# Turning the last two query batches on VectorE, and cutting later loads into rows, in a fused attention and two-MLP kernel

## The chip, the cores and the metric

One core of one Trainium2 chip runs the whole program. The metric is the device time of one execution in microseconds. Three runs of the kernel before gave 1151.23, 1151.44 and 1151.57 us.

## The reference, cut to what matters

```python
# q, k, v: (4, 8, 576, 64); phi: (4, 8, 576, 32)
a = softmax(phi over the sequence)
k_m, v_m = einsum(a, k), einsum(a, v)            # 32 memory slots a head
attn = softmax(scale * q @ k_m.T)
x = (attn @ v_m), heads side by side              # (2304, 512)
h = x @ w_in;  x = leaky_relu(h, 0.01) @ w_out    # w_in, w_out are float64
p = domain_probs / domain_probs.sum(-1)
out = sum over 4 experts of p[:, e] * (relu(x @ w1[e]) @ w2[e])
```

## The kernel before, in words

The program has three stages. **Attention** goes batch by batch, four batches, named 0 to 3 here. A batch takes phi's maxima with a tree of four VectorE additions (`tree`, L548), turns them with two TensorE transposes (L552, L558), subtracts (L560) and exponentiates on ScalarE (L563). It turns its queries with 20 TensorE transposes (L576), whose results ScalarE or VectorE copy out of PSUM (L344). It forms the 32 memory keys and values with 72 small matmuls (L607; L596 for the values of batch 0), sums the weights with a second tree (L548, the z tree) and one matmul (L619), turns keys and values (L662, L658), and then, for each half s of the tokens, makes scores with 16 small matmuls (L685) and a softmax on VectorE (transposes out of PSUM L697, maxima L704, L706, exponent L709, sums L711, L713, L717, transposes back L720). The probabilities are split into a rounded high part and a low part (L344, L347); these are the tokens `ah`, `al`.

**The first MLP** folds the memory values into w_in: `y_pair` (L976) makes a y, which ACT and DVE split (L344, L347). `moe1_step` multiplies tokens and y in six matmuls (L960; for the first two steps three and three), applies the leaky rectifier (L1015), splits (L344, L347) and does twelve matmuls with w_out (L1027 to L1029). Its weights are float64 in memory and come as pieces of 512 values a partition, two 32-bit words a value. `piece64` makes float32 of them: a high part on ScalarE (L861) shifted on DVE (L879), a low part (L865 on ScalarE, L867 on DVE), the sign put into the low word (`signs`, L873 on DVE), and an addition on GpSimd (L878).

**The second MLP** (L1136 to L1206) takes the rest, from about 390 us on.

While attention runs, a region `xx` of four rows of 2304 words a partition holds the loads: `X0` to `X3` are its four quarters, each 576 words in each of the four rows. Keys, values and the queries of batch 1 live there; `A0` is elsewhere and holds the other queries. The fourth to seventh weight piece (`more0` to `more3`) is also kept in `xx`, one in each row, in words 1152 to 2175, that is in X2 and X3. Values of batch 1 go to X1.

The order on every engine comes from a planner (`Plan.issue`): each step has an engine, a cost and a due time, and a list scheduler writes them out; a table `SHIFTS` moves the due times of numbered steps. While TensorE has nothing in the plan during the first 50 us, the planner writes filler matmuls (L481) on the unit matrix. The engines run in that order, and wait on semaphores that a recorder adds from what the steps read and write. DMAs take eight semaphores, DMAHW0 to DMAHW7, in turn, and one that takes a semaphore waits for the DMA that had it last.

Of the kernel before, what the change touches and what calls it, by code (L numbers as in the profile page):

```python
# [11 lines left out]
F32R = mybir.dt.float32r  # L12
U32 = mybir.dt.uint32
F16 = mybir.dt.float16
AF = mybir.ActivationFunctionType
ALU = mybir.AluOpType
# [171 lines left out]
def kernel(  # L188
# [26 lines left out]
    HG = 4  # L215
# [314 lines left out]
    def att_batch(b):  # L530
# [10 lines left out]

        def tree(fold, rows):
            h = rows.shape[1]
            half = [tops[:, 0:n * P].rearrange("p (h r m) -> p h r m", h=h, r=n) for n in (4, 2, 1)]
            pairs = [(half[0], rows[:, :, 0:4], rows[:, :, 4:8]), (half[1], half[0][:, :, 0:2], half[0][:, :, 2:4]),
                     (half[2], half[1][:, :, 0:1], half[1][:, :, 1:2]), (half[2], half[2], rows[:, :, 8:9])]
            for out, in0, in1 in pairs:
                nc.vector.tensor_tensor(out=out, in0=in0, in1=in1, op=fold)  # L548
        op("DVE", 1.75, due, lambda: tree(ALU.max, rows), ["pl"], ["aT1"], two=True)
# [16 lines left out]
        due = yield  # L566
        for part in range(3):
            pairs = range(2 * part, min(2 * part + 2, (LT + 1) // 2))
            rows_, n = P if part < 2 else D, len(pairs) * HG * P
            pq = Banks(psum, (n + 511) // 512)  # L570

            def fn(pq=pq, pairs=pairs, rows_=rows_):
                for i, pair in enumerate(pairs):
                    for h in range(HG):
                        at_p = (i * HG + h) * P
                        nc.tensor.transpose(  # L576
                            pq[at_p:at_p + P][0:rows_], home(qn)[:, h, 2 * pair * D:2 * pair * D + rows_], ident)
            op("PE", 0.11 * len(pairs) * HG + 0.1, due, fn, [qn, "ident"], [pq], room=[f"qT{part}"])
            op("ACT", act(n), due, lambda e, pq=pq, pairs=pairs, rows_=rows_, n=n: copy(
                e, qT[0:rows_, pairs[0]:pairs[-1] + 1].rearrange("p r h n -> p (r h n)"), pq[0:n][0:rows_]),  # L580
               [pq], [f"qT{part}"], also=("DVE", dve(n)))

        for names in (("k",), ("v",)) if b == 0 else (("k", "v"),):
# [7 lines left out]
            def fn(pkv=pkv, src=src, n=len(names), wide=wide):  # L591
                for r in range(LT):
# [11 lines left out]
                    for h in range(HG):  # L604
                        for g in range(NGB):
# [7 lines left out]
                            )  # L613
            op("PE", 4.3 if wide else 1.0 + 0.6 * len(names), due, fn, ["a"] + [HOME[nm][b] for nm in names], [pkv])
            if "k" in names:
                op("DVE", 1.75, due, lambda: tree(ALU.add, a.rearrange("p r h m -> p r (h m)").unsqueeze(1)),
                   ["a"], ["aT1"], two=True)
                pz = Banks(psum, 1)
# [33 lines left out]
            for nm in names:  # L652
                pk = Banks(psum, 1)

                def fn(pk=pk, nm=nm):
                    if nm == "v":
                        for g in range(NGB):
                            nc.tensor.matmul(pk[0:P][g * D:(g + 1) * D], lhsT=kv[:, g, 1], rhs=ident, start=True, stop=True)  # L658
                        return
                    for x in range(2):  # L660
                        for g in range(NGB):
                            nc.tensor.matmul(pk[g * P:(g + 1) * P][x * D:(x + 1) * D],  # L662
                                             lhsT=kv[:, g, 0], rhs=ident, start=True, stop=True)
                n = 2 if nm == "k" else 1
# [8 lines left out]
        for s in range(2):  # L673
# [4 lines left out]
            def fn(ps=ps, s=s):  # L678
                for g in range(NGB):
                    for h in range(HG):  # L680
                        for x in range(2):
                            n = (LT + 1 - x) // 2
                            at_x = x * 512 + g * n * M
                            rs = slice(x * D, (x + 1) * D)
                            nc.tensor.matmul(  # L685
                                ps[at_x:at_x + n * M][h * M:(h + 1) * M].rearrange("p (r t) -> p r t", t=M),
                                lhsT=kb[rs, g, h * M:(h + 1) * M],
                                rhs=qT[rs, 0:n, h, (2 * g + s) * M:(2 * g + s + 1) * M],
                                start=True,
                                stop=True,  # L690
                            )
            op("PE", 0.7, due, fn, ["qT0", "qT1", "qT2", "kb"], [ps], [f"at{s}"])
# [7 lines left out]
            op("DVE", dve(S) + 0.15, due, fn, [ps, f"one{s}"], [f"at{s}"])  # L700
            at_r = at_[:, :, 0:M]
# [143 lines left out]
    def piece64(kind, n, sl, src, due, key, after):  # L845
# [23 lines left out]
        def signs(e):  # L869
            if e == "ACT":  # L870
                nc.scalar.mul(raw.bitcast(F16)[..., 1::4], high.bitcast(F32), 2.0 ** -112)
            else:
                nc.vector.scalar_tensor_tensor(  # L873
                    out=low, in0=high, scalar=0x80000000, in1=low, op0=ALU.bitwise_and, op1=ALU.bitwise_or
                )

# [4 lines left out]
        plan.op("ACT", 0.57, due, rest, [], [rk], also=("DVE", 0.5), two=True)  # L881
        plan.op("DVE", 0.7, due, signs, [], [rk], also=("ACT", 1.36), two=True)
        plan.op("POOL", 1.3, due, lambda e: add(e, fu), [rk], [fk], also=("DVE", 1.0), two=True)
# [78 lines left out]
    def y_pair(t, m, n):  # L962
# [25 lines left out]
        plan.op("PE", 0.45 * n - 0.1, t, fn,  # L988
                [key for i in range(n) for key in w_keys("w1", p + i)] + [f"vt{b * NGB + g}" for g in range(NGB)],
# [304 lines left out]
```

## Time and profile before

| | |
|---|---|
| median of 3 runs | 1151.44 us (1151.23 to 1151.57) |
| profiled execution, its own time | 1151.32 us |
| its span, first to last instruction | 1149.5 us |
| mean granted TensorE clock | 0.996 |
| busy: PE / DVE / ACT / POOL | 1127.0 / 676.2 / 440.5 / 98.2 us |
| HBM read / written | 125.60 / 34.08 MB |

Busy times are sums over an engine's instructions. PE counts matmuls, PEld the weight loads that overlap them. A busy PE is not a PE at its peak, since its fillers count, and since a matmul at half clock takes twice as long. The chain of waits follows the work back from the last instruction.

### The profile page before, as it was taken

The page shows a single profiled execution, that of the slowest core. Times are in us where ns is not written, and L with a number is a line of the kernel's source. Part 1 is how long each engine was busy: PE and PEld are TensorE (multiplying, and loading weights), DVE is VectorE, ACT ScalarE, POOL GpSimd, SP SyncE. Part 2 cuts the span into 40 slices and gives each one's busy share as a digit, 9 for nine tenths or more (in the row PEclk, how much of TensorE's full clock was granted, in tenths as well). Part 3 has the DMA queues.
Part 4 walks back from the last instruction along what each step waited for, and adds up shares of the span by engine and source line. Part 5 has one row for each costly group of instructions (what it writes and reads, how often), then busy time and mean ns, then how long its engine had stood idle before and what let it go on. Part 6 is the DMA issues. An engine that isn't in the chain of part 4 may idle for free.

```text
span 1149.5 us, 18174 instructions
## 1 busy us (share of the span) xinstructions
PE 1127.0 (98%) x7420; PEld 1020.6 (89%) x7420; DVE 676.2 (59%) x1279; ACT 440.5 (38%) x893; POOL 98.2 (9%) x102
## 2 busy tenths in 40 slices
PE   7699999999999999999999999999999999999998
PEld 4579999999999998989898998999998989998897
DVE  5776475843345787668677644455376644454543
ACT  5555567743434544433333323222124223222220
POOL 2431125510000000000000000000000000000000
PEclk9899999999999999999999999999999999999999
DMA  9555013310000377444544644433344553344402
GB/s 349 203 180 161 1 38 130 111 38 1 2 19 17 104 272 278 163 163 196 201 183 147 193 174 165 160 136 130 152 165 165 156 205 131 140 165 165 165 19 56
DMA packets 54104, 160.86 MB, mean 140 GB/s; under 512 B 6148, under 2 KB 22532, under 8 KB 47876
## 3 DMA queue, kind: packets, MB, share of 16 engines
q1 hardware_dynamic: 48836, 100.19, 24.8%
q0 software_dynamic: 4608, 58.72, 14.4%
q8 instruction: 58, 0.95, 0.3%
q10 hardware_dynamic: 576, 0.79, 0.2%
q14 instruction: 26, 0.21, 0.1%
HBM read 125.60 MB, written 34.08 MB: 139 GB/s over the span
## 4 chain that ended last, share of the span: by engine, by line
PE 95%; DMA 2%; DVE 2%; issue 0%; SPq 0%; ACT 0%; POOL 0%; DVEq 0%
PE psum L1136 31%; PE psum L1206 12%; PE psum L1205 12%; PE psum L1204 11%; PE psum L960 9%; PE psum L1027 6%; PE psum L1029 6%; PE psum L1028 6%; PE psum L976 1%; DMA exact<-in_moe_w_out_dram 1%; DMA exact<-in_v_dram 1%; PE psum L576 1%; PE psum L607 1%; PE psum L685 0%; DVE exact L873 0%
## 5 line engine op out<-in xcount | busy, mean ns | idle before, releaser
L1145 DVE TENSOR_TENSOR exact<-psum,exact 128x384 f32<-128x384 f32 x336 | 184.1, 556 | 272.0 <-PE psum L1136 269.6
L1152 ACT ACTIVATE rounded<-exact 128x384 fp32r<-128x384 f32 x192 | 100.9, 525 | 292.8 <-DVE exact L1145 291.0
L347 DVE TENSOR_TENSOR rounded<-exact,rounded 128x288 fp32r<-128x288 f32 (+3 forms) x223 | 123.5, 569 | 102.7 <-ACT rounded L344 101.9
L1206 PE MATMUL psum<-late,rounded 128*128 128x512 f32 x384 | 150.7, 392 | 0.0
L1205 PE MATMUL psum<-late,rounded 128*128 128x512 f32 x384 | 150.5, 392 | 0.0
L1204 PE MATMUL psum<-late,rounded 128*128 128x512 f32 x384 | 149.3, 389 | 0.0
L1136 PE MATMUL psum<-rounded 128*128 128x384 f32 x768 | 143.6, 336 | 0.1
L1136 PEld LDWEIGHTS psum<-rounded 128*128 128x128 f32 x768 | 134.8, 188 | 3.1 <-DVE exact L1145 1.0
L960 PE MATMUL psum<-rounded 128*128 128x288 f32 x768 | 125.4, 300 | 7.9 <-DVE rounded L347 7.9
L960 PEld LDWEIGHTS psum<-rounded 128*128 128x128 f32 x768 | 110.1, 191 | 14.0 <-issue 11.7
L344 ACT CAST rounded<-exact 128x288 fp32r<-128x288 f32 (+2 forms) x240 | 115.2, 500 | 14.1 <-DVE exact L820 3.9
L1027 PE MATMUL psum<-rounded 128*128 128x288 f32 x384 | 115.7, 301 | 0.0
L1029 PE MATMUL psum<-rounded 128*128 128x288 f32 x384 | 113.2, 295 | 2.3 <-issue 2.3
L1028 PE MATMUL psum<-rounded 128*128 128x288 f32 x384 | 113.2, 295 | 0.0
L1136 PE MATMUL psum<-late,rounded 128*128 128x384 f32 x576 | 109.7, 336 | 0.0
L1156 DVE SCALAR_TENSOR_TENSOR rounded<-exact,rounded 128x384 fp32r<-128x384 f32 x192 | 98.8, 550 | 12.9 <-ACT rounded L1152 12.9
L1136 PEld LDWEIGHTS psum<-late,rounded 128*128 128x128 f32 x576 | 102.0, 188 | 3.8
L1015 ACT ACTIVATE exact<-psum 128x288 f32<-128x288 f32 x128 | 52.6, 411 | 131.2 <-PE psum L960 126.6
L1167 ACT COPY exact<-psum 128x384 f32<-128x384 f32 x48 | 23.1, 481 | 196.8 <-PE psum L1136 196.8
L1206 PEld LDWEIGHTS psum<-late,rounded 128*128 128x128 f32 x384 | 72.0, 188 | 15.1
L1205 PEld LDWEIGHTS psum<-late,rounded 128*128 128x128 f32 x384 | 72.0, 188 | 13.4
L1204 PEld LDWEIGHTS psum<-late,rounded 128*128 128x128 f32 x384 | 72.1, 188 | 13.2
(113 smaller groups left out, 1664.6 us busy)
## 6 DMA issues: line engine op xcount, KB each, us to landing
rounded<-kept POOLq DMA_DIRECT2D x22, 1792.0 KB, 7.6
exact<-in_moe_w_dram SPq DMA_DIRECT2D x64, 512.0 KB
kept<-rounded SPq DMA_DIRECT2D x10, 1792.0 KB
w<-kept POOLq DMA_DIRECT2D x10, 1792.0 KB, 7.5
kept<-w SPq DMA_DIRECT2D x6, 1792.0 KB
exact<-in_moe_w_in_dram SPq DMA_DIRECT2D x16, 512.0 KB
exact<-in_moe_w_out_dram SPq DMA_DIRECT2D x16, 512.0 KB
exact<-in_k_dram SPq DMA_DIRECT2D x4, 1152.0 KB
```

The costliest lines, as they stand in the source:

```text
L344: nc.scalar.copy(out, in_) if e == "ACT" else engine(e).tensor_copy(out, in_)
L347: engine(e).tensor_tensor(out=out, in0=in0, in1=in1, op=ALU.subtract)
L960: nc.tensor.matmul(ps, lhsT=l, rhs=r, start=start and n == 0, stop=stop and n == len(seq) - 1)
L1027: nc.tensor.matmul(po, lhsT=w2l[:, ds_], rhs=th, start=first, stop=False)
L1028: nc.tensor.matmul(po, lhsT=w2h[:, ds_], rhs=tl, start=False, stop=False)
L1029: nc.tensor.matmul(po, lhsT=w2h[:, ds_], rhs=th, start=False, stop=last)
L1136: nc.tensor.matmul(ps[k][0:TB], lhsT=l, rhs=r, start=(i == 0), stop=(i == 5))
L1145: plan.op("DVE", dve2(TB), at[k], lambda: nc.vector.tensor_tensor(out=o, in0=ps[k][0:TB], in1=other, op=ALU.add), [ps[k], ok, from_], [key])
L1152: plan.op("ACT", act2(TB), at[k], lambda: nc.scalar.activation(out=th, in_=src, func=AF.Relu), [key, *h_from[hs[c, i]]], [keys[0]])
L1204: nc.tensor.matmul(po[0:DM], lhsT=tl, rhs=w2h[:, c], start=(p == 0 and c == 0), stop=False)
L1205: nc.tensor.matmul(po[0:DM], lhsT=th, rhs=w2l[:, c], start=False, stop=False)
L1206: nc.tensor.matmul(po[0:DM], lhsT=th, rhs=w2h[:, c], start=False, stop=(p == NP2 - 1 and c == 1))
```

## The change: what it does

- Batches 2 and 3 (the third and fourth; `TURNED` names the first two) turn their queries with one VectorE transpose of 32x32 blocks each (2304 values a partition) in place of 20 TensorE transposes and three copies. For these the memory keys are turned into 32-row pieces with eight matmuls in place of four, and a half's 16 score matmuls contract 32 rows and send 288 columns, two accumulating into one result, in place of 64 rows and 160 or 128 columns. One transpose takes them out of PSUM in place of two. The score matmuls of all batches are issued in another order.
- Loads into `xx` for batches 1 to 3 are four transfers, one for each row, in place of one.
- `signs` on DVE masks the upper 16 bits of each high word into the upper half of the low word, one operand, in place of an instruction with two operands on 32-bit words.
- The z trees of batches 1 to 3 may go to GpSimd.
- The loads of `domain_probs`, 24 small ones, come after attention.
- Two costs of the planner change (memory matmuls, y), and `SHIFTS` is another table, which reorders the steps of the first 160 us, loads and weight pieces included.

```diff
-SHIFTS = [
-    (553, 34, 1.0), (417, 30, 3.4), (490, 3, -13.8), (250, 28, -6.7), (643, 12, -17.4), (245, 9, -18.3),
-    (528, 3, -41.5), (100, 1, -9.4), (318, 30, 112.8), (316, 28, -7.4), (601, 12, -7.9),
-]
+SHIFTS = [(256, 12, -56.2), (398, 28, 5.8), (564, 30, -19.6), (114, 1, 6.4), (12, 12, -41.5), (520, 1, -16.2), (571, 32, -4.0), (224, 1, 12.7), (409, 4, -23.9), (266, 30, 2.5), (248, 1, -2.2), (72, 2, 7.0), (442, 1, 4.9), (320, 12, 2.6), (453, 1, 35.3), (293, 30, -1.6), (438, 1, 4.2), (96, 4, -29.5), (505, 4, 3.9), (243, 12, -19.1)]
...
+    TURNED = (0, 1)
...
+    qD = qT.rearrange("p a h n -> p (a h n)")[:, 0:HG * LT * D].rearrange("p (h c e t) -> p h c e t", h=HG, c=LT, e=2)
...
-        plan.op("SP", 3.0, due, lambda: nc.sync.dma_start(
-            out=home(name), in_=src[b].rearrange("h s d -> (h s d)").rearrange("(h p w) -> p h w", h=HG, p=P)),
-            writes=[name])
+        from_ = src[b].rearrange("h s d -> (h s d)").rearrange("(h p w) -> p h w", h=HG, p=P)
+
+        def fn():
+            for hs in [slice(h, h + 1) for h in range(HG)] if name[0] == "X" and b else [every]:
+                nc.sync.dma_start(out=home(name)[:, hs], in_=from_[:, hs])
+        plan.op("SP", 3.0, due, fn, writes=[name])
...
+        else:
+            op("DVE", 2.5, due, lambda: nc.vector.transpose(
+                out=qD.rearrange("p h c e t -> p (h c e t)"), in_=home(qn)), [qn], ["qT0", "qT1", "qT2"])
...
+                    op("DVE", 1.75, due, lambda e, total=total: total(e=e), ["a"], ["aT1"], also=("POOL", 3.0), two=True)
...
+                    for e in range(2):
+                        for w in range(2 * NGB):
+                            nc.tensor.matmul(pk[e * P:(e + 1) * P][w * M:(w + 1) * M],
+                                             lhsT=kv[:, w // 2, 0, e * M:(e + 1) * M], rhs=ident, start=True, stop=True)
...
+                            else:
+                                rs = slice((2 * g + s) * M, (2 * g + s + 1) * M)
+                                out_ = ps[g * 512:g * 512 + HB][h * M:(h + 1) * M]
+                                lhsT, rhs = kb[rs, x, h * M:(h + 1) * M], qD[rs, h, :, x]
+                            nc.tensor.matmul(out_, lhsT=lhsT, rhs=rhs, start=turned or x == 0, stop=turned or x == 1)
...
-        plan.op("SP", 2.0, 150.0 + 4 * t_, partial(load_probs, t_), [], ["probs"])
+        plan.op("SP", 2.0, 150.0 + 4 * t_, partial(load_probs, t_), ["attention"], ["probs"])
...
-                nc.vector.scalar_tensor_tensor(
-                    out=low, in0=high, scalar=0x80000000, in1=low, op0=ALU.bitwise_and, op1=ALU.bitwise_or
-                )
+                halves = raw.bitcast(U16)
+                nc.vector.tensor_single_scalar(halves[..., 1::4], halves[..., 3::4], 0x8000, op=ALU.bitwise_and)
```

**DVE, around the signs of two weight pieces kept in `xx`.** The program counts its DMAs through eight semaphores, so a name in brackets tells which DMA is waited for: before, the values of batch 1 are the sixteenth DMA and count on DMAHW7. L873 (now L896) is `signs`, L347 (L346) a low part, L697 (L719) the scores out of PSUM. Before:

```order
L720 STREAM_TRANSPOSE att<-att 128x576 [waits DVE_49]
L879 TENSOR_SCALAR w_63<-w_63 128x2x256
L879 TENSOR_SCALAR exact<-exact 128x512
L347 TENSOR_TENSOR rounded<-att,rounded 128x2x288 [waits Activation_49]
L873 SCALAR_TENSOR_TENSOR exact<-exact 128x512 [waits DMAHW7_49,DMAHW0_49]
L873 SCALAR_TENSOR_TENSOR exact<-exact 128x512 [waits DMAHW1_49]
L347 TENSOR_TENSOR rounded<-psum,rounded 128x512 [waits PE_49]
L697 STREAM_TRANSPOSE att<-psum 128x2x5x32 [waits Pool_49]
```

And now:

```order
L742 STREAM_TRANSPOSE att<-att 128x576 [waits DVE_49]
L896 TENSOR_SCALAR exact<-exact 128x512 [waits DMAHW3_49,Activation_49]
L896 TENSOR_SCALAR exact<-exact 128x512 [waits DMAHW1_49]
L346 TENSOR_TENSOR rounded<-psum,rounded 128x512 [waits Activation_49]
L719 STREAM_TRANSPOSE att<-psum 128x2x5x32
L719 STREAM_TRANSPOSE att<-psum 128x2x4x32 [waits DVE_49]
L346 TENSOR_TENSOR rounded<-att,rounded 128x2x288 [waits Activation_49]
L900 TENSOR_SCALAR w_63<-w_63 128x2x256
```

The signs no longer wait for the values of batch 1, only for their own pieces (DMAHW3 and DMAHW1 are those of their loads now), and the low part of the first tokens comes behind them, after the scores' two transposes.

**SP, from the second load of phi to the keys of batch 1.** L526 (now L530) loads q, k or v, L521 phi, L162 (L160) a weight piece, L400 the probabilities. Before:

```order
L521 DMA att<-in_phi_dram 128x4x288 [waits DMAHW5_49]
L162 DMA exact<-in_moe_w_out_dram 128x1024 [waits DMAHW6_49,Pool_49]
L526 DMA exact<-in_v_dram 128x4x576 [waits PE_49,DMAHW7_49,Activation_49,Pool_49]
L526 DMA att<-in_q_dram 128x4x576 [waits DMAHW0_49]
L400 DMA exact<-in_moe2_domain_probs_dram 128x1x4 [waits DMAHW1_49]
L400 DMA exact<-in_moe2_domain_probs_dram 128x1x4 [waits DMAHW2_49]
L526 DMA exact<-in_q_dram 128x4x576 [waits DMAHW3_49,Activation_49,Pool_49]
L526 DMA exact<-in_k_dram 128x4x576 [waits DMAHW4_49]
```

And now, from the values of batch 1:

```order
L530 DMA exact<-in_v_dram 128x576 [waits PE_49]
L530 DMA exact<-in_v_dram 128x576 [waits DMAHW7_49]
...
L160 DMA exact<-in_moe_w_in_dram 128x2x512 [waits DMAHW2_49,Pool_49]
L530 DMA att<-in_q_dram 128x4x576 [waits DMAHW3_49]
L530 DMA exact<-in_q_dram 128x576 [waits DMAHW4_49,Pool_49]
L530 DMA exact<-in_q_dram 128x576 [waits DMAHW5_49,DVE_49]
...
L530 DMA exact<-in_k_dram 128x576 [waits DMAHW0_49]
```

The values of batch 1 wait for TensorE alone (the values of batch 0 have been read), no longer for ACT and POOL, and stand as four transfers; the probabilities are gone from between the loads.

## Rows read from the trace of the kernel before

**Rows 1.** The page: busy time by engine; granted clock in 40 slices.

```profile
PE 1127.0 (98%) x7420; PEld 1020.6 (89%) x7420; DVE 676.2 (59%) x1279; ACT 440.5 (38%) x893; POOL 98.2 (9%) x102
...
PEclk9899999999999999999999999999999999999999
```

**Rows 2.** The page: chain that ended last, share of the span by engine.

```profile
PE 95%; DMA 2%; DVE 2%; issue 0%; SPq 0%; ACT 0%; POOL 0%; DVEq 0%
```

**Rows 3.** Busy us by stretch: length, PE, PEld, DVE, ACT, POOL, PEclk, DMA, GB/s.

```profile
20.00:40.00 20.00, 11.77 (x129) 6.18 (x126) 14.70 (x28) 11.96 (x23) 6.94 (x5) 0.85 0.75 274
40.00:60.00 20.00, 17.69 (x256) 14.75 (x255) 18.26 (x29) 12.96 (x23) 11.26 (x8) 0.98 0.64 220
60.00:80.00 20.00, 17.65 (x181) 15.03 (x182) 14.84 (x27) 10.46 (x24) 6.46 (x5) 0.91 0.60 213
...
80.00:160.00 80.00, 80.00 (x1023) 73.37 (x1021) 49.91 (x94) 46.29 (x103) 13.83 (x11) 1.00 0.18 59
```

**Rows 4.** Waits of PE, whole span: us in total, times, longest.

```profile
PE psum L960 <- DVE rounded L347: 7.9, 2, 7.2
...
PE psum L1029 <- issue: 2.3, 1, 2.3
```

**Rows 5.** The chain in order of time, 26 to 37 us: start, us, what.

```profile
26.09 1.31 POOL w L878
...
27.41 7.39 DMA exact<-in_v_dram
...
34.90 1.29 DVE exact L873 x2
...
36.94 1.79 PE psum L960 x6
```

**Rows 6.** Timeline of DVE, 28 to 38 us: start, us, what.

```profile
28.06 0.78 DVE L720 STREAM_TRANSPOSE att<-att 128x576 f32<-128x576 f32 x1
...
29.58 0.76 DVE L347 TENSOR_TENSOR rounded<-att,rounded 128x576 fp32r<-128x576 f32 x1
...
36.11 0.68 DVE L347 TENSOR_TENSOR rounded<-psum,rounded 128x512 fp32r<-128x512 f32 x1
36.71 0.99 DVE L697 STREAM_TRANSPOSE att<-psum 128x320 f32<-128x320 f32 x2
```

**Rows 7.** The chain in order of time, batch 2 and the y of that time.

```profile
91.78 0.87 PE psum L576 x8
...
92.77 1.31 PE psum L576 x12
...
104.80 0.72 PE psum L685 x25
...
113.77 1.02 PE psum L976 x16
...
121.31 0.59 PE psum L976 x16
```

**Rows 8.** Groups by form, 0 to 170 us: busy us, mean ns, idle before.

```profile
L873 DVE SCALAR_TENSOR_TENSOR exact<-exact 128x512 uint32<-128x512 uint32 x16 | 12.1, 764 | 7.9 <-DMA exact<-in_v_dram 4.6 <-ACT exact L865 3.0
...
L879 DVE TENSOR_SCALAR w<-w 128x512 uint32<-128x512 uint32 x8 | 3.3, 415 | 0.3 <-ACT w L861 0.3
L720 DVE STREAM_TRANSPOSE att<-att 128x576 f32<-128x576 f32 x4 | 3.1, 772 | 0.0
```

**Rows 9.** Timeline of DVE, two neighbouring low parts of the first MLP.

```profile
109.04 0.46 DVE L347 TENSOR_TENSOR rounded<-exact,rounded 128x288 fp32r<-128x288 f32 x1 [0.57 <-ACT rounded L344]
...
113.97 0.41 DVE L347 TENSOR_TENSOR rounded<-exact,rounded 128x288 fp32r<-128x288 f32 x1
```

**Rows 10.** The chain at 61 us, and two stretches at half clock (columns of rows 3).

```profile
61.38 2.35 issue
...
34.00:41.00 7.00, 4.06 (x28) 3.01 (x29) 5.44 (x10) 2.21 (x5) 3.70 (x3) 0.51 0.20 66
...
64.75:68.16 3.41, 3.41 (x21) 3.08 (x18) 2.84 (x4) 0.79 (x2) 1.35 (x2) 0.50 1.04 397
```

More of the change, by code (lines that the diff above doesn't have):

```diff
@@ L13 @@
 U32 = mybir.dt.uint32
+U16 = mybir.dt.uint16
 F16 = mybir.dt.float16
@@ L540, in att_batch, with tree @@
         due = yield
-        def tree(fold, rows):
+        def tree(fold, rows, e="DVE"):
             h = rows.shape[1]
@@ L547, in tree @@
             for out, in0, in1 in pairs:
-                nc.vector.tensor_tensor(out=out, in0=in0, in1=in1, op=fold)
+                engine(e).tensor_tensor(out=out, in0=in0, in1=in1, op=fold)
         op("DVE", 1.75, due, lambda: tree(ALU.max, rows), ["pl"], ["aT1"], two=True)
@@ L566, in att_batch, with fn @@
         due = yield
[L567 to L581, printed above, removed]
+        turned = b in TURNED
+        if turned:
+            for part in range(3):
+                pairs = range(2 * part, min(2 * part + 2, (LT + 1) // 2))
+                rows_, n = P if part < 2 else D, len(pairs) * HG * P
+                pq = Banks(psum, (n + 511) // 512)
+                def fn(pq=pq, pairs=pairs, rows_=rows_):
+                    for i, pair in enumerate(pairs):
+                        for h in range(HG):
+                            at_p = (i * HG + h) * P
+                            nc.tensor.transpose(
+                                pq[at_p:at_p + P][0:rows_], home(qn)[:, h, 2 * pair * D:2 * pair * D + rows_], ident)
+                op("PE", 0.11 * len(pairs) * HG + 0.1, due, fn, [qn, "ident"], [pq], room=[f"qT{part}"])
+                op("ACT", act(n), due, lambda e, pq=pq, pairs=pairs, rows_=rows_, n=n: copy(
+                    e, qT[0:rows_, pairs[0]:pairs[-1] + 1].rearrange("p r h n -> p (r h n)"), pq[0:n][0:rows_]),
+                   [pq], [f"qT{part}"], also=("DVE", dve(n)))
+        else:
+            op("DVE", 2.5, due, lambda: nc.vector.transpose(
+                out=qD.rearrange("p h c e t -> p (h c e t)"), in_=home(qn)), [qn], ["qT0", "qT1", "qT2"])
         for names in (("k",), ("v",)) if b == 0 else (("k", "v"),):
@@ L613, in fn @@
                             )
-            op("PE", 4.3 if wide else 1.0 + 0.6 * len(names), due, fn, ["a"] + [HOME[nm][b] for nm in names], [pkv])
+            op("PE", 4.3 if wide else 2.1 if b == 0 else 3.0, due, fn, ["a"] + [HOME[nm][b] for nm in names], [pkv])
             if "k" in names:
-                op("DVE", 1.75, due, lambda: tree(ALU.add, a.rearrange("p r h m -> p r (h m)").unsqueeze(1)),
-                   ["a"], ["aT1"], two=True)
+                total = partial(tree, ALU.add, a.rearrange("p r h m -> p r (h m)").unsqueeze(1))
+                if b == 0:
+                    op("DVE", 1.75, due, total, ["a"], ["aT1"], two=True)
+                else:
+                    op("DVE", 1.75, due, lambda e, total=total: total(e=e), ["a"], ["aT1"], also=("POOL", 3.0), two=True)
                 pz = Banks(psum, 1)
@@ L659, in fn @@
                         return
[L660 to L663, printed above, removed]
+                    if turned:
+                        for x in range(2):
+                            for g in range(NGB):
+                                nc.tensor.matmul(pk[g * P:(g + 1) * P][x * D:(x + 1) * D],
+                                                 lhsT=kv[:, g, 0], rhs=ident, start=True, stop=True)
+                        return
+                    for e in range(2):
+                        for w in range(2 * NGB):
+                            nc.tensor.matmul(pk[e * P:(e + 1) * P][w * M:(w + 1) * M],
+                                             lhsT=kv[:, w // 2, 0, e * M:(e + 1) * M], rhs=ident, start=True, stop=True)
                 n = 2 if nm == "k" else 1
@@ L699, in fn @@
                         in_=ps[x * 512:x * 512 + NGB * n * M].rearrange("p (w c t) -> p w c t", w=NGB, t=M))
-            op("DVE", dve(S) + 0.15, due, fn, [ps, f"one{s}"], [f"at{s}"])
+            op("DVE", dve(S) + 0.15 * turned, due, fn, [ps, f"one{s}"], [f"at{s}"])
             at_r = at_[:, :, 0:M]
@@ L881, in piece64 @@
         plan.op("ACT", 0.57, due, rest, [], [rk], also=("DVE", 0.5), two=True)
-        plan.op("DVE", 0.7, due, signs, [], [rk], also=("ACT", 1.36), two=True)
+        plan.op("DVE", 0.42, due, signs, [], [rk], also=("ACT", 1.36), two=True)
         plan.op("POOL", 1.3, due, lambda e: add(e, fu), [rk], [fk], also=("DVE", 1.0), two=True)
```

29 lines of the change are left out of this document (15 added, 14 removed).

## The prediction, made before the changed kernel was run

> **What bounds the kernel now.** I read the page first, then busy time by stretch, PE's waits, the chain in order of time, and the timeline of DVE. PE is busy for 1127.0 of 1149.5 us and carries 95% of the chain [rows 1, 2]: time comes off only where PE has less to do, or stops waiting. The stretches say where each can be. From 80 us on PE never rests (80.00 of 80.00 us, [rows 3]), so there a microsecond of PE work saved is a microsecond saved. Before 80 us PE idles: 8.2 us between 20 and 40 us, 2.3 and 2.35 us in the next two stretches [rows 3], and part of its busy time there is filler. Two waits stand out: 7.2 us of L960, the first product of the first MLP, on a DVE low part, and 2.3 us in which PE waits for nothing shown [rows 4].
>
> The chain tells what is behind the first [rows 5]: GpSimd's L878 ends at 27.40, the load of v is issued at 27.41 and takes 7.39 us, DVE's two signs start at 34.90, PE at 36.94. Signs of a weight piece have no use for v. The order shows why they wait: that v goes to X1, four strips 2304 words apart, and the pieces sit between these strips; the wait is one on a load that spans them without touching them. DVE had finished its last work at 29.58 + 0.76 = 30.34 [rows 6] and then waited 4.6 us [rows 8]. The load itself waited for GpSimd's work on such a piece, the same mistake the other way round.
>
> **The change, part by part.** The sum is against the profiled execution: its own 1151.32 us is 1.8 us above its span and 0.1 below the median.
>
> *Loads by row, and the new order.* Each of the four transfers now covers one strip, and the order shows neither signs waiting for v nor v for GpSimd. I rebuild DVE's queue from the end of L720 at 28.84 [rows 6]; what stands ahead of it is one signs in place of one, and one shift more (0.42) against a signs shorter by 0.27, which I call even. Behind it now come two signs, the low part of the first y (0.68), two transposes out of PSUM (0.99), the low part of the tokens (0.76) [rows 6]. With signs at 0.42 that is 28.84 + 0.84 + 0.68 + 0.99 + 0.76 = 32.1, and PE's first full product starts then, not at 36.94: 4.8 us earlier; with signs as slow as now (0.65 each, [rows 5]) 4.3. Bounds: nothing, if a later load holds PE instead, and 7.2 us, the whole wait. I take 4.5, near the 4.6 us that DVE waited. What is late next is the same chain of DVE and ACT between 37 and 50 us that is there now (DVE is busy 18.26 of 20 us, [rows 3]); it only starts sooner. It needs phi, q and k of batch 1. Their loads lose the two small loads of probabilities that stood ahead of q and k. Those move behind attention and cost nothing: they are wanted by the second MLP, and DMA is 0.18 busy between 80 and 160 us [rows 3].
>
> *Signs.* Two operands of 512 values took 0.65 to 0.76 us, one operand 0.42 [rows 5, 8]. The new form reads every fourth half word; between 0.42 and 0.69 I take 0.42, since it is a one-operand form as L879 is. On the chain before 80 us I count one more, 0.3 us; after 80 us DVE has room (49.91 of 80, [rows 3]) and it is worth nothing.
>
> *Queries turned by DVE.* On PE this removes 0.87 + 1.31 = 2.18 us of transposes a batch [rows 7], 4.36 for two, in the stretch where PE never rests. What the scores cost instead: y's eight matmuls, on eight sub-arrays at once, take 1.02 us at 512 columns and 0.59 at 256 [rows 7], so 1.68 ns a column and 0.16 fixed. A half's 16 score matmuls now put 2 x 288 = 576 columns on each of eight sub-arrays: 0.16 + 0.97 = 1.13, where 320 took 0.72 [rows 7]. That is 0.41 more, 1.64 for two halves of two batches. If the 32-row sub-arrays of the two groups don't overlap, the columns double: 2.1 us each, 5.5 more in all; if all overlapped better than now, nothing more. I take 1.6. Turning the keys sends 256 columns through each of four sub-arrays, as before: even. Net: -2.7 us (between -4.4 and +1.1).
>
> On DVE it adds a transpose of 2304 values: 576 take 0.77 [rows 8], so between 1.9 (at the 512 in 0.42 of L879) and 3.1 us (four times 576). It drops one copy. DVE is in order, and behind the transpose wait low parts that PE needs. But there are now 4.9 us between two such low parts at 109 to 114 us [rows 9], and PE didn't rest: 3.1 us are covered. Without that cover it would cost up to 2 x 3.1. The copies that ACT is spared hide behind PE now.
>
> *z trees.* The new order has no tree on POOL: this part costs and gives nothing. *Scores of batches 0 and 1 in another order*: the same columns on the same sub-arrays, even.
>
> *The clock.* After the 7.2 us of idling PE ran at 0.51 between 34 and 41 us, with 4.06 us of work [rows 10], of which 1.79 are the first product on the chain [rows 5]. At full clock 0.9 of it would be saved. The new plan has eight filler matmuls where there were twelve, so PE still idles before its first product, and I count none of it.
>
> Sum: 1151.3 - 4.5 - 0.3 - 2.7 = **1143.8 us**.
>
> **Rivals.**
>
> *The start is given back.* The time won at 32 us is lost again to q and k of batch 1, and only PE's saving and the signs are left: 1151.3 - 0.3 - 2.7 = 1148.3, between 1147 and 1150 with the bounds of the scores. For it: the eight semaphores are used up twice as fast, and the first strip of q still waits for GpSimd's work on a piece. Against: GpSimd's work comes earlier too, since its signs do.
>
> *The stall without a cause goes too.* At 61.38 PE stops for 2.35 us while the load queues are full, and runs at half clock from 64.75 to 68.16 [rows 10]: 2.35 + 1.7 = 4.0 us. With the loads and PE's order moved it may not come: 1143.8 - 4.0 = 1139.8. Against: it comes soon after the 72 small memory matmuls of batch 1, and in the new order these too are followed by the loads for batches 2 and 3.
>
> *Slower: the strips are carried one after another.* A load of 1152 KB took 7.39 us [rows 5], of which the bytes, at 397 GB/s [rows 10], are 3.0; the other 4.4 are waiting and handling. If every strip paid that, a load would take 4 x (4.4 + 0.75) = 20.6 us, 13 more; batch 1's memory matmuls wait for q and k, eight strips, so up to 26 us more: 1143.8 + 26 = 1169.8. It decides from some 2.8 us a strip on, where two loads are 7.5 us late. Against: the order has the strips waiting on DMAs eight places back, not on each other, so eight can be under way. The Trainium skill (DMA: Bandwidth & Descriptors, Rules for kernel authors) speaks against this change too: it wants many small transfers joined into one, and large ones of 1 MiB or more. Its section Anatomy of one DMA gives about 2.0 us fixed for each; as an estimate from it, 3 more a load, paid in turn, would be 6 us a load, 12 for two. No run here shows yet whether strips overlap.
>
> *Slower: no overlap of 32-row sub-arrays at all.* Sixteen matmuls in turn are 16 x 288 x 1.68 ns = 7.7 us in place of 0.72, 7.0 more for each of four halves: 1151.3 - 4.5 - 0.3 - 4.4 + 28.1 = 1170.2. It decides from 3.0 us a half on. Against: eight 64-row sub-arrays do overlap [rows 7].
>
> **How the numbers follow.** The forecast gets 0.54, the stall's going 0.14, the start given back 0.20, the two slower ones 0.07 together; 0.05 is for a gain eaten up otherwise. A measurement of this kernel can tell some 0.2%, 2.3 us, from no change: faster means below 1149.1. The first two and 0.11 of the third are faster, 0.79; 0.14 the same; 0.07 slower. The range reaches from 1139.3, the stall gone, to 1149.0, the start given back with dear scores; some 0.2 lies outside, nearly all of it above.
>
> **What would show it.** In the profile after: no DVE wait on v, PE's first L960 product (now L981) at 31 to 33.5 us; signs at about 0.42 us; per batch 2 and 3 no PE transposes of queries, scores near 1.1 us a half, one DVE transpose of 2 to 3 us and PE without rest from 80 us; a chain still 95% PE. Wrong would be: PE waiting 2 us or more for q, k or v of batch 1 or behind the long transpose, scores of 2 us or more, or a first product at 36 us again.

## The result, and the profile after

Four runs of the changed kernel gave a median of 1139.29 us (1139.04 to 1140.76); four of the kernel before gave 1151.34 (1149.44 to 1151.57). The ratio is 0.9902, with a 95% interval of 0.9884 to 0.9919: shorter by 12.05 us, about 1%, where 7.5 were forecast. The direction was right; the median stands right at the low end of the range, 1139.3.

The profiled execution took 1140.76 us, the longest of the four, with a span of 1139.0 us. The others had spans of 1137.2 to 1137.6 us at a mean granted clock of 0.998 to 1.000, where it had 0.997. Only this execution was traced; by these means the others had less of the stretch at half clock that is shown below, or none. So the two profiled executions stand 10.5 us apart, and the medians 12.05.

The page of the changed kernel, to be held against [rows 1, 2]:

```profile
PE 1121.1 (98%) x7388; PEld 1014.5 (89%) x7388; DVE 679.7 (60%) x1270; ACT 437.4 (38%) x890; POOL 102.5 (9%) x106
...
PEclk9899999999999999999999999999999999999999
...
PE 95%; DVE 2%; DMA 2%; SPq 0%; issue 0%; POOL 0%; ACT 0%; DVEq 0%
```

TensorE still carries 95% of the chain, and is busy for 5.9 us less (fillers and time at half clock are in this sum). The stretches of [rows 3], in the changed kernel:

```profile
20.00:40.00 20.00, 15.24 (x150) 9.52 (x146) 18.67 (x34) 14.66 (x28) 10.13 (x8) 0.83 0.90 323
40.00:60.00 20.00, 17.19 (x259) 14.70 (x258) 17.08 (x29) 12.33 (x24) 9.05 (x8) 1.00 0.75 250
60.00:80.00 20.00, 20.00 (x225) 17.24 (x224) 16.78 (x26) 14.42 (x34) 10.82 (x9) 1.00 0.43 157
80.00:160.00 80.00, 80.00 (x1005) 71.69 (x1004) 52.15 (x91) 43.86 (x102) 15.79 (x12) 1.00 0.19 60
```

TensorE's idle time falls from 8.2 to 4.8 us in the first stretch, is 2.8 in the second (2.3 before), and falls from 2.35 us to nothing in the third. The waits of TensorE from 20 to 160 us, against [rows 4]:

```profile
PE psum L981 <- DVE rounded L346: 2.4, 2, 1.4
PE psum L981 <- ACT exact L887: 1.7, 1, 1.7
PE psum L997 <- ACT exact L343: 1.0, 1, 1.0
```

The 7.2 us ahead of the first full product have become 1.7 and 1.1, and the 2.3 us in which TensorE waited for nothing shown are gone. VectorE's timeline from 26 to 33 us (before: [rows 6]) shows why the first went:

```profile
26.30 0.74 DVE L896 TENSOR_SCALAR exact<-exact 128x512 uint16<-128x512 uint16 x1
...
29.18 0.78 DVE L742 STREAM_TRANSPOSE att<-att 128x576 f32<-128x576 f32 x1
29.88 1.28 DVE L896 TENSOR_SCALAR exact<-exact 128x512 uint16<-128x512 uint16 x2
30.96 0.70 DVE L346 TENSOR_TENSOR rounded<-psum,rounded 128x512 fp32r<-128x512 f32 x1
31.58 0.98 DVE L719 STREAM_TRANSPOSE att<-psum 128x320 f32<-128x320 f32 x2
32.49 0.72 DVE L346 TENSOR_TENSOR rounded<-att,rounded 128x576 fp32r<-128x576 f32 x1
```

No wait on v stands ahead of the two signs. The same row shows what did not come true: two signs, one starting before the other has ended, take 1.28 us, as before (1.29), and the single one at 26.30 takes 0.74. A single one of the old form, in the kernel before:

```profile
25.33 0.68 DVE L873 SCALAR_TENSOR_TENSOR exact<-exact 128x512 uint32<-128x512 uint32 x1
```

Signs, the new transposes and the scores in full, first by groups of one form (0 to 170 us), then the chain in order of time around batch 2:

```profile
L896 DVE TENSOR_SCALAR exact<-exact 128x512 uint16<-128x512 uint16 x18 | 15.7, 882 | 0.7
...
L588 DVE STREAM_TRANSPOSE att<-att 128x2304 f32<-128x2304 f32 x2 | 5.1, 2565 | 0.0
```

```profile
94.37 0.57 PE psum L679 x16
94.94 0.37 PE psum L669 x4
...
97.09 1.18 PE psum L708 x29
...
103.23 1.16 PE psum L708 x29
```

A sign costs 882 ns in the mean, where the old form's mean was 764 [rows 8]; both means carry a few that took 1.9 to 2.0 us (two of the 18, one of the 16). A half of scores (L708) takes 1.18 and 1.16 us where it took 0.72 [rows 7]. The stretch at half clock (columns of [rows 3]), in this execution:

```profile
32.52:39.35 6.83, 6.09 (x36) 5.00 (x37) 6.05 (x11) 4.43 (x9) 4.42 (x5) 0.50 0.63 198
61.30:69.00 7.70, 7.70 (x110) 6.84 (x109) 6.19 (x11) 4.14 (x12) 3.60 (x3) 1.00 0.73 275
```

The first of before's two stretches is still there in this execution; the second, behind the stall at 61 us, is not.

### The profile page after: what moved, and what is told of

Same layout as the page of the kernel before. It is cut to its first block, busy times and chain, and to the rows that moved or that the text cites. A ratio compares the mean times of both kernels' runs of the same rounds, so it can differ in the third digit from the quotient of the medians.

```text
span 1139.0 us, 18144 instructions
## 1 busy us (share of the span) xinstructions
PE 1121.1 (98%) x7388; PEld 1014.5 (89%) x7388; DVE 679.7 (60%) x1270; ACT 437.4 (38%) x890; POOL 102.5 (9%) x106
## 4 chain that ended last, share of the span: by engine, by line
PE 95%; DVE 2%; DMA 2%; SPq 0%; issue 0%; POOL 0%; ACT 0%; DVEq 0%
PE psum L1157 31%; PE psum L1227 12%; PE psum L1226 12%; PE psum L1225 11%; PE psum L981 9%; PE psum L1048 6%; PE psum L1050 6%; PE psum L1049 6%; PE psum L997 1%; DMA exact<-in_moe_w_out_dram 1%; PE psum L708 1%; DVE exact L896 0%; DVE exact L551 0%; PE psum L615 0%; DMA exact<-in_k_dram 0%
## 5 line engine op out<-in xcount | busy, mean ns | idle before, releaser
L346 DVE TENSOR_TENSOR rounded<-exact,rounded 128x288 fp32r<-128x288 f32 (+2 forms) x222 | 126.0, 582 | 101.1 <-ACT rounded L343 100.1
L981 PE MATMUL psum<-rounded 128*128 128x288 f32 x768 | 124.1, 298 | 4.2 <-DVE rounded L346 2.4
L343 ACT CAST rounded<-exact 128x288 fp32r<-128x288 f32 (+4 forms) x239 | 114.7, 501 | 13.0 <-DVE exact L842 4.6
L981 PEld LDWEIGHTS psum<-rounded 128*128 128x128 f32 x768 | 109.4, 190 | 8.5 <-issue 5.6
```

Source lines behind the costliest of these rows:

```text
L343: nc.scalar.copy(out, in_) if e == "ACT" else engine(e).tensor_copy(out, in_)
L346: engine(e).tensor_tensor(out=out, in0=in0, in1=in1, op=ALU.subtract)
L981: nc.tensor.matmul(ps, lhsT=l, rhs=r, start=start and n == 0, stop=stop and n == len(seq) - 1)
```

## The experiments

Two theories stood at the start. By the first, three things make up the gain: the loads' false wait, a stall that had nothing to do with the change's parts as such, and TensorE's saving in batches 2 and 3. By the second it is the new order of work. Times are medians, beside runs of the kernel before on the same chip; before's median lay between 1150.94 and 1151.7 us there. The changed kernel was not run beside them, so differences to its 1139.29 are good to about 1 us.

### Loads by row alone, and everything but them

On the kernel before:

```diff
-        plan.op("SP", 3.0, due, lambda: nc.sync.dma_start(
-            out=home(name), in_=src[b]...), writes=[name])
...
+        def fn():
+            for hs in [slice(h, h + 1) for h in range(HG)] if name[0] == "X" and b else [every]:
+                nc.sync.dma_start(out=home(name)[:, hs], in_=from_[:, hs])
+        plan.op("SP", 3.0, due, fn, writes=[name])
```

> The kernel before, with one part of the change alone: the loads of batches 1 to 3 go in four transfers, one a row of heads; the order of all work stays. Theory A (the false wait on v of batch 1 and what follows from it is the larger part of the gain): VectorE no longer waits 4.6 us for v of batch 1, the first full product of the first layer begins 3.5 to 5 us earlier than at 36.94, and the run is 4 to 8 us shorter than before: 4 if the stall without a cause at 61.38 stays, 8 if it goes as well. Rival B (it is the new order of the work, and the rows alone do nothing): the product comes within 1 us of its old place or the start is given back by 80 us, and the time stays within 1 us of 1151.3.

1145.97 us against 1150.94, ratio 0.9954 (0.9942 to 0.9967): 5.0 us less. TensorE's waits, 0 to 160 us:

```profile
PE psum L963 <- DVE rounded L347: 3.2, 2, 2.5
PE psum L1031 <- issue: 1.8, 1, 1.8
```

The 7.2 us ahead of the first product are 2.5, and the product begins at 32.33 us, 4.6 earlier. The stall without a shown cause is still there, 1.8 us long, and the second stretch at half clock did not come. Theory A, with the stall staying. Between the two profiles the six products at 60.08 us of before stand 4.4 us earlier, and those from 71 us on 6.35: some 2 us belong to the shorter stall and the clock behind it. (This profiled execution, 1144.92 us, is one of the shorter ones.)

The other way round, on the changed kernel:

```diff
-            for hs in [slice(h, h + 1) for h in range(HG)] if name[0] == "X" and b else [every]:
+            for hs in [slice(h, h + 1) for h in range(HG)] if False else [every]:
```

> The changed kernel, with the loads of batches 1 to 3 in one transfer each again; everything else of the change stays. Theory A: VectorE waits for v of batch 1 again, and 4 to 8 us of the 12 come back: 1143 to 1147 us. Rival B (the new order is what starts TensorE sooner): below 1141 us.

1145.22 us, ratio 0.9954 (0.994 to 0.9967): 5.9 above the changed kernel. Its chain in order of time:

```profile
26.45 5.47 DMA exact<-in_v_dram
...
35.53 1.28 DVE exact L896 x2
...
38.93 1.09 PE psum L981 x3
```

The load of v is back on the chain, and the products begin late again. The new order alone does not start TensorE sooner. Still the run is 5.7 us shorter than before: the queries stay on VectorE, and the stall at 61 us does not come here either (its waits from 20 to 160 us have no "issue").

### Queries of batches 2 and 3 on TensorE again

On the changed kernel, with the table of shifts kept on the same steps:

```diff
-    TURNED = (0, 1)
+    TURNED = (0, 1, 2, 3)
```

> The changed kernel, with the queries of batches 3 and 4 turned by TensorE again, as those of batches 1 and 2, and with the scores in their old form; the other parts and the new order stay. By the prediction's sum this gives back 2.7 us (4.36 us of transposes less 1.64 of slower scores). Theory A: 2.0 to 3.0 us slower than the changed kernel, TensorE's busy sum in 80 to 160 us unchanged because it is full there either way. Rival C (VectorE's turning costs TensorE waits or the evictions' cover elsewhere): less than 1 us slower. Rival D (the stall at 61.38 went because of this part): over 4 us slower.

1141.40 us, ratio 0.992 (0.9907 to 0.9934): 2.1 us above the changed kernel. Theory A; the term was 2.7.

### The order of before

On the changed kernel, with the old table put on the same steps as in the kernel before. The planner's new costs stay: besides those of the memory matmuls and of y, the costs of the signs and of the scores are new too.

```diff
-SHIFTS = [(256, 12, -56.2), (398, 28, 5.8), ...
+SHIFTS = [(553, 34, 1.0), (417, 30, 3.4), ...
```

> The changed kernel with the table of shifts of the kernel before (put on the same steps as there): all parts of the change, without its new order. Theory A (the order itself is worth little: rows, queries on VectorE and the lost stall make the gain): within 2 us of the changed kernel. Rival B (the gain rests on the order): 4 us slower or more, with TensorE waiting longer ahead of 60 us.

1144.70 us, ratio 0.9946 (0.9934 to 0.9959): 5.4 above the changed kernel, so theory A fell for this part. TensorE's timeline there:

```profile
51.52 0.66 PE L1004 MATMUL psum<-w,exact 64*32 64x256 f32 x16
55.05 0.35 PE L637 MATMUL psum<-att,exact 128*128 128x2 f32 x2 [2.87 <-DVE exact L557]
...
56.55 3.79 PE L622 MATMUL psum<-exact,att 64*32 64x128 f32 x144
```

and in the changed kernel:

```profile
50.60 0.95 PE L997 MATMUL psum<-w,exact 64*32 64x256 f32 x16
52.10 2.24 PE L615 MATMUL psum<-exact,att 64*32 64x128 f32 x144 [0.55 <-ACT att L566]
55.71 1.85 PE L981 MATMUL psum<-rounded 128*128 128x288 f32 x12 [1.37 <-DVE rounded L346]
```

With the old table the sum z of batch 1 (L637) stands ahead of the burst of 72 memory matmuls, and TensorE waits 2.87 us for VectorE's tree of sums; the burst then runs at half clock (0.50 from 56.49 to 59.90 us) and takes 3.79 us where it took 2.24. The new table has z behind the burst (L630, at 57.80). So the order is worth 5.4 us *given the other parts*. It isn't a saving by itself: with one load a transfer it gave none at the start, and the kernel before, with its own table, had no wait of this kind.

### What the stall at 61 us is

TensorE stood for 2.35 us at 61.38 with nothing shown that it waited for [rows 10]. The page lists a queue of kind "instruction", with 58 packets of 0.95 MB in all. TensorE's products and weight loads together are 14,840 [rows 1], so some 256 to a packet of 16 KB; such a packet's instructions are called a block here. Kernel before, DMA queues in two neighbouring windows, 57 to 61.3 us and 61.3 to 62.4 us (packets, MB, share of 16 engines; a share can pass 100%, since a packet counts whole where it starts):

```profile
q1 hardware_dynamic: 911, 1.49, 95.8%
...
q1 hardware_dynamic: 153, 0.32, 85.2%
q8 instruction: 1, 0.02, 5.7%
```

The burst of memory matmuls, 288 instructions, runs from 57.66. During it the queue brings no instructions; the next packet comes as TensorE stops. Two edits that leave all useful work as it is ask whether the stall is this. The first adds instructions that do nothing of use, among fillers in TensorE's idle time (27 small matmuls of four instructions each; the second kernel has 10 and 11 in place of 4 and 5, 63 in all):

```diff
     def idle(bank):
         nc.tensor.matmul(psum[:, bank]..., lhsT=ident, rhs=ident..., start=True, stop=True)
+        for _ in range((4, 5)[idles[0] % 2] if 3 <= idles[0] < 9 else 0):
+            nc.tensor.matmul(psum[0:32, bank][:, 0:2], lhsT=ident[:, 0:32], rhs=ident[:, 0:2], start=True, stop=True)
+        idles[0] += 1
```

> The kernel before with 27 more matmuls of 32 x 2 elements (108 instructions of TensorE) among the fillers in its idle time ahead of the first full product; no other work, wait or load is changed. It asks what the 2.35 us at 61.38 are in which TensorE waits for nothing. Theory F (TensorE has run through the instructions it has, and the transfer that brings the next 256 comes late): the burst of small matmuls at 57.7 then falls on another part of a block, the stall is below 0.5 us or lies elsewhere, and with it goes the stretch at half clock behind it: 1147 to 1149. Rival G (the stall belongs to that place in the program, a product's bank or a matmul of it): it stays at 2.0 to 2.5 us at the same matmul and the time stays within 1 us of 1151.3.

> The same with 63 more matmuls (252 instructions, nearly one whole block of 256), so that the burst falls on the same part of a block as before. Theory F: the stall is back within 0.2 us of TensorE's time of the same matmul, 1.5 to 2.5 us long, and the time is within 1.5 us of 1151.3. Rival H (any filler that keeps TensorE in motion in the idle time ahead of 37 us removes the stall or the half clock behind it): no stall, and at least 2 us less than before.

With 108 more: 1149.50 us, ratio 0.9975 (0.9965 to 0.9985). At 61 us nothing stalls, nor does the half clock come behind it, and TensorE is 3.4 us ahead of before from 72 to 92 us. But the burst of batch 2 now falls on the bad part of a block, and a stall comes there:

```profile
94.60 2.18 PE L612 MATMUL psum<-exact,att 64*32 64x128 f32 x136
98.19 0.42 PE L612 MATMUL psum<-exact,att 64*32 64x128 f32 x8 [1.41 <-issue]
```

That takes 1.8 us of the 3.4 back, so the time missed the expected 1147 to 1149 by half a microsecond. With 252 more, almost a whole block: 1150.96 us, ratio 0.9993 (0.9985 to 1.0002), and the stall is back behind the burst, two products further on:

```profile
64.39 0.29 PE L1033 MATMUL psum<-rounded 128*128 128x288 f32 x1 [2.47 <-issue]
```

The instructions that TensorE had run when it stopped can be counted (columns of [rows 3]), in the kernel before and with 252 more:

```profile
0.00:61.38 61.38, 45.69 (x600) 31.86 (x601) 42.95 (x80) 33.54 (x59) 21.89 (x27) 0.94 0.78 283
```

```profile
0.00:62.00 62.00, 51.40 (x728) 35.95 (x729) 43.67 (x81) 33.90 (x60) 22.41 (x27) 0.97 0.79 282
```

That is 1201 and 1457: 256 apart, one block, though 252 were added. With TensorE's few semaphore instructions counted in, it stops behind record 1217 before, 1473 with 252 more, and 2241 with 108 more, which is 1217 and four blocks. With loads by row it stops behind 1218. In each of these the next product starts 1.3 to 1.4 us after the packet's last byte.

Theory F; the place in the program (G) and the fillers' motion (H) are out. The second edit moves no instruction of TensorE. The order of calls is collected, and three loads are put behind the two loads of weights that wait until 65 us:

```diff
...
-                    fn(e) if len(engines) > 1 else fn()
+                    order.append((n, e, partial(fn, e) if len(engines) > 1 else fn))
...
+        held = [o for o in order if o[0] in self.held]
+        queue = [i for i, o in enumerate(order) if o[1] == "SP"]
+        last = max(i for i, o in enumerate(order) if o[0] in self.held)
+        to = order[queue[queue.index(last) + 4]]
+        order = [o for o in order if o[0] not in self.held]
+        to = order.index(to) + 1
+        for _, _, fn in order[:to] + held + order[to:]:
+            fn()
...
+        if (what, b) in (("v", 3), ("v", 2), ("k", 2)):
+            plan.held.add(len(plan.ops) - 1)
```

> The kernel before with three loads later in SyncE's queue: v of batch 3, v and k of batch 2, issued behind the two loads of first-layer weights that wait until 65.4 us. TensorE's instructions are the same in number and order. Theory F1 (the transfer of TensorE's instructions comes late because it stands behind those loads): with no load in flight at 57 to 63 us it starts less than 1.5 us after the burst begins, the stall at 61.38 is below 0.7 us, and the run is 2 to 4 us shorter. Theory F2 (it comes late whatever else is moved): the stall stays within 0.5 us of 2.35 and the time within 1 us. If batch 2's values come too late by this, TensorE waits for them ahead of its products of batch 2 at about 98 us, which neither theory expects.

1147.77 us against 1151.70, ratio 0.9959 (0.9946 to 0.9973): 3.9 us less by the order of three loads alone (between the profiles 0.8 us of it lies ahead of 37 us). The queues from 57 to 58.5 and from 58.5 to 59.6 us, and TensorE at the old place of the stall:

```profile
q1 hardware_dynamic: 545, 0.51, 105.6%
...
q1 hardware_dynamic: 136, 0.23, 67.3%
q8 instruction: 1, 0.02, 5.0%
```

```profile
60.99 0.29 PE L1041 MATMUL psum<-rounded 128*128 128x288 f32 x1 [0.43 <-issue]
```

The packet comes some 1.7 us after the burst's start at 56.85, where it came 3.7 after it (61.3 less 57.66); 1.5 had been expected, with no load in flight; but earlier loads fill the queues until 58.5, and the packet starts at 58.52, as they thin out. 0.43 us of the stall are left. So two things make it: a burst that uses up a block, and loads that the next block stands behind (F1).

### Both edits of loads together

The kernel before, with loads by row and the three loads later.

> The kernel before with the two edits of loads that gained alone put together: loads of batches 1 to 3 in four transfers, one a row of heads (5.0 us alone), and v of batch 3, v and k of batch 2 issued behind the two loads of weights that wait until 65 us (3.2 to 3.9 us alone). TensorE's, VectorE's, ScalarE's and GpSimd's instructions are those of before in their order. Theory A (the false wait and the late transfer of instructions are separate): 7 to 9 us less than before, 1142 to 1144, with the stall below 0.7 us, and the change's other parts have 3 to 5 us left to explain. Rival B (both take from one and the same slack): 5 to 6 us less than before.

1143.35 us, ratio 0.9936 (0.9922 to 0.9949): 7.85 us less, with the stall at 0.5:

```profile
PE psum L1043 <- issue: 0.5, 1, 0.5
```

Theory A, a microsecond short of the sum of the two (8.9). One reason shows in the runs: with loads by row the half clock behind the stall was gone already.

### Parts that were worth nothing

The signs in their old form, on the changed kernel:

```diff
-                halves = raw.bitcast(U16)
-                nc.vector.tensor_single_scalar(halves[..., 1::4], halves[..., 3::4], 0x8000, op=ALU.bitwise_and)
+                nc.vector.scalar_tensor_tensor(
+                    out=low, in0=high, scalar=0x80000000, in1=low, op0=ALU.bitwise_and, op1=ALU.bitwise_or
+                )
```

> The changed kernel with the signs in their old form, one instruction over 32-bit words with two operations, the order of all work unchanged. The profile of the changed kernel has the new form at 0.64 to 0.75 us for 128x512, as the old one had. Theory A (the signs' new form gains nothing): within 0.8 us of the changed kernel, the old form at 0.64 to 0.76 us. Rival B (the new form saves time that its row doesn't show, because it holds the port shared with GpSimd for less): over 1 us slower, and GpSimd's additions of halves longer than in the changed kernel.

1139.41 us, ratio 0.989 (0.9877 to 0.9904): the same as the changed kernel. The group by form, 0 to 170 us:

```profile
L895 DVE SCALAR_TENSOR_TENSOR exact<-exact 128x512 uint32<-128x512 uint32 x18 | 14.6, 817 | 0.8 <-ACT exact L887 0.5
```

817 ns in the mean against 882, each with two of about 1.9 us among 18: the new form gains nothing on its row either. Theory A by the time; the mean lies above the 0.64 to 0.76 us that it named.

The loads of probabilities, on the changed kernel:

```diff
-        plan.op("SP", 2.0, 150.0 + 4 * t_, partial(load_probs, t_), ["attention"], ["probs"])
+        plan.op("SP", 2.0, 150.0 + 4 * t_, partial(load_probs, t_), [], ["probs"])
```

> The changed kernel with the loads of the probabilities free to go ahead of the end of attention again, as before the change; the planner then orders part of the work otherwise. Theory A (holding them back is worth nothing by itself, small loads that stand beside large ones): within 1 us of the changed kernel. Rival B (in SyncE's queue they stand ahead of loads that TensorE needs): over 1.5 us slower, with a wait of TensorE on a load of batch 1 to 3 ahead of 110 us.

1139.37 us, ratio 0.990 (0.9884 to 0.9917): the same as the changed kernel. Theory A.

### A try at something faster

On the changed kernel:

```diff
-    WARM, PART, IDLE, SHORT = (5.0, 50.0), 0.7, 0.95, 1.0
+    WARM, PART, IDLE, SHORT = (5.0, 50.0), 1.1, 0.95, 1.0
```

> The changed kernel with more of the fillers that keep TensorE in motion while it waits ahead of the first full product: seven in place of four in the wait at 26 us, three in place of two at 8 us. The changed kernel's TensorE ran at half clock from 32.5 to 39.4 us after that wait. Theory A (the wait is what the half clock answers to): the stretch is shorter or gone, the first products are no later than 33.3 us, and the run is 1 to 3 us shorter than the changed kernel: 1136.5 to 1138.5. Rival B (the fillers only stand in the way, or the products of batch 1 wait for VectorE's maxima at 44 us anyway, so what the clock gives is waited away): within 1 us of the changed kernel.

1139.22 us, ratio 0.990 (0.9885 to 0.9915): no gain over the changed kernel's 1139.29. In its profile TensorE held the clock where the changed kernel's had lost it:

```profile
32.52:39.35 6.83, 5.91 (x50) 4.87 (x51) 5.92 (x11) 4.93 (x10) 4.75 (x4) 1.00 0.64 204
```

Its span is 1137.4 us, that of the changed kernel's other executions. By the time it is rival B, by the clock theory A; but that the fillers kept the clock is not shown, since two of the changed kernel's four executions had a mean clock of 1.000 without them. And the stall is back, as its waits from 20 to 160 us show:

```profile
PE psum L1048 <- issue: 0.5, 1, 0.5
```

It falls behind the same 1217th record of TensorE. No version here beats the changed kernel.

## Why the prediction was right, and where it fell short

**The range and the forecast.** The direction and the parts that were priced came out, but the forecast, 1143.8, is 4.5 us above the median, and that the range holds 1139.29 rests on its rounded end: this is luck. What the sum lacked is the stall at 61 us, which it kept, and some of the clock.

**What bounds the kernel** was read rightly: the gain lies in the first 150 to 160 us, in TensorE's idle time, its clock and its work. From there on the two executions run alike: the same product of the first MLP comes 9.9 us earlier at 151 us of before, and still 9.9 at 401 us. The chain is 95% TensorE after as before.

**Loads by row, -4.5.** Right, in mechanism and size: VectorE's wait on v is gone, the first full products begin at 31.8 and 33.3 us (31 to 33.5 were named), and the edit by itself gave 5.0 us; in its profile the earlier start is worth 4.4 at 60 us, and the rest is the shorter stall and the clock. The part "and the new order" was mis-sized: it was costed as nothing beyond this start. The run with the old table shows 5.4 us that hang on it, a wait of 2.87 us for z's tree and a burst at half clock, which the other parts would have brought without it.

**Signs, -0.3.** Wrong, and small. The step that failed is "between 0.42 and 0.69 I take 0.42, since it is a one-operand form as L879 is". L879 goes over 32-bit words without a gap, the signs over every fourth half word. The pair at 29.88 took 1.28 us with GpSimd idle, as long as the old form's pair in [rows 5], and one by itself 0.74. The row to lean on was the old form's, whose steps through memory are as long; the bound's other end, 0.69, was nearly right. That the steps are the reason was not tried by itself. The first product still came in time, since what the 0.42 was to gain was a quarter of a microsecond each.

**Queries on VectorE, -2.7.** Right in mechanism: 2.1 by the run that undoes it. Scores were 1.16 to 1.18 us a half where 1.13 was worked out, so 0.1 to 0.2 of the term is there; the rest, some 0.4 us, is within what such runs scatter. One transpose took 2.57 us, inside 1.9 to 3.1, and TensorE did not rest from 60 us on: the cover of 4.9 us held.

**z trees, 0.** As costed: GpSimd got none.

**The clock, 0.** As said, some idle time ahead of the first products stayed (1.7 and 1.1 us), and a half-clock stretch in the profiled execution. The executions with a higher mean clock have spans 1.4 to 1.8 us shorter, part of the 12.05 that no step had counted.

**The rivals.** "The stall without a cause goes too" came true on top of the forecast; it was given 0.14 and gave 1139.8, half a microsecond from what was measured. It was kept low for the wrong reason: that loads follow the burst in the new order too. They do (DMA is 0.91 to 1.10 busy in each microsecond from 55 to 65 us of the changed kernel's trace), but the stall needs the burst to run out of its block as well. In the changed kernel the packet of instructions starts at 55.66 us, 3.6 after the burst's start at 52.10 and so as late as before. But TensorE gets to the same 1218th record only at 59.08, 7.0 us after the burst's start, where it took 3.7 before: it waits 1.37 us for a low part (the row of L981 at 55.71), and 29 more records lie between. The run with more fillers has the same wait, but its burst stands 16 records closer to that place, and there 0.5 us of stall came. So the wait alone does not keep the stall away; how much of the rest is the place and how much the loads was not tried. The start was not given back. Both slower cases fell: with 288 KB strips no wait of TensorE for q, k or v of batch 1 of 2 us or more came, and sixteen score matmuls on 32-row sub-arrays overlap (1.17, not 7.7 us).

The Trainium skill's rule (DMA: Bandwidth & Descriptors, Rules for kernel authors) asks for 1 MiB or more in a transfer, for bandwidth, and for many small ones to be joined. That was not what counted here: cutting one of 1152 KB into four of 288 KB gained 5.0 us, ratio 0.9954, because in this program a transfer that spans other tiles is waited for by their users. That strips would be carried one after another no run shows: with loads by row TensorE waited at most 0.5 us for a load. (The 2.0 us that the prediction took from that page's section Anatomy of one DMA is stated there for DMAs issued from GpSimd, while these are SyncE's.)

**How 12.05 comes together:** 7.85 by the two edits of loads (loads by row, stall with its half clock), 2.1 by the queries, and 2.1 left over. This is a comparison and not a taking apart, since the changed kernel does not hold the second edit; in it the stall is gone by its own order. What is left over is not settled by a run of its own: the rest of the order, the planner's costs, the score matmuls of batches 0 and 1 in another order, and the half clock that some executions have are all in it.

## What to carry to other kernels

A tile that lies in strips between other tiles can be waited for, as here, by all that lies between; give each strip its transfer, and look at the order for waits on loads that an instruction has no use for. Where an engine stops and the profile names nothing, look at the queue of kind "instruction" in narrow windows: a burst of hundreds of small instructions ahead of full load queues can run dry, and moving three loads behind it gained 3.9 us here. Fillers move such a place too, for better or worse. When costing a new form of an instruction, take the row with the same steps through memory rather than the one with the same number of operands.

## What was not expected of the hardware

TensorE can stand for lack of instructions: 2.35 us here, 1.8 with loads by row, 1.41 in another place with 108 instructions more, back at 2.47 with 252, and 0.43 with the loads out of the way. It stops behind the same record each time, or a whole number of 256 further on. The cost can be more than the stall, since TensorE ran at half clock after the two longest: from 64.75 to 68.16 us, 3.41 us at 0.50, in the kernel before. And a pass over every fourth half word of 128x512 with one operand took 0.74 us by itself, and 882 ns in the mean, no less than the 32-bit form with two operands (0.68, and in the changed kernel 817 in the mean).
